# Queries of the linear-attention layers: two row blocks at a time instead of one, in a new order of steps

## The chip, the cores and the metric

The kernel runs on one core of one Trainium2 chip. The metric is the device time of one execution in microseconds (us), as the median of several runs; lower is better. The granted TensorE clock is 1.000 in the profiled execution.

## The reference

Four layers follow one another on one sequence of 2048 rows with 512 columns, in bfloat16: kind A, kind B, kind A, kind B. Each adds its result to its input, and each starts with a layer norm without weights.

```
def _A_ref(x, wqkv, wo):            # first kind: linear attention, 32 heads of 16
    q, k, v = heads(x @ wqkv)
    phi = lambda t: where(t > 0, t + 1, exp(t)) + 1e-6
    pq, pk = phi(q), phi(k)
    kv  = einsum("bhsd,bhse->bhde", pk, v)      # sum over all rows
    z   = einsum("bhsd->bhd", pk)
    num = einsum("bhqd,bhde->bhqe", pq, kv)
    den = einsum("bhqd,bhd->bhq", pq, z) + 1e-6
    return merge(num / den) @ wo

def _B_ref(x, wqkv, wo):            # second kind: causal softmax attention, window of 256 rows
    ...
x = x + _A_ref(_layernorm(x), A_wqkv, A_wo)
x = x + _B_ref(_layernorm(x), B_wqkv, B_wo)
x = x + _A_ref(_layernorm(x), A_wqkv, A_wo)
x = x + _B_ref(_layernorm(x), B_wqkv, B_wo)
```

The sum `kv` runs over all rows, so no output of a layer of the first kind can be formed before all 2048 rows have gone into it. This barrier occurs twice.

## The kernel before

The 2048 rows are cut into 16 row blocks of 128 (`t` = 0 to 15). All activations stay in SBUF: `xres[t]` is the residual stream of block t. The kernel is written as a list of steps (`_Sched.op`), each with an engine, what it reads and writes, and a closure that issues its instructions. `graph` builds the list:

- Part "1.": for each block, `a_kv` does layer norm (`ln`), a transpose of the normed block into `xTa`, the keys `k` with their feature map (`phi`) and the values `v`; `kv_mm` adds the block's product to the sum in PSUM. `sums` (steps `fin0`, `fin1`, L1220) masks the finished sum into `kvz`: the first barrier.
- `segment("2.", ...)`: for each block `a_q` forms the queries of the first layer, `a_out` multiplies them with `kvz` (steps `n0`, `n1`, L942), divides and projects by `Ao` into `xres`; then `b_qkv` and `b_attn` do the second layer on the block. `b_attn` computes scores in units of two pairs of PSUM banks; ScalarE takes the exponential of 1024 columns per pair into `pF` (L1077) or `pH` (L1035); VectorE masks; TensorE multiplies with the values (L1113, L1125).
- Part "2k.": `a_kv` again for the third layer, with the second barrier (`2.fin0`, `2.fin1`) at its end; then `segment("3.", ...)` does the third and fourth layers in the same way.

`a_q` before, for one block: `proj_feat` issues 16 matmuls of 128 columns (steps `q0`, `q1`, L870) into one PSUM bank; `phi` then has four steps on 512 columns: `q.e`, the exponential on ScalarE from PSUM (L879); `q.m`, minimum with 1 and plus 1e-6 on VectorE (L880); `q.r`, the rectifier on ScalarE from PSUM (L882); `q.a`, the sum of both on VectorE (L883). The result lies in one of 18 buffers `pq`.

Work of different blocks and layers is interleaved. What stands in the queue of each engine, and in which order, is fixed by the text `ORDER`: a list of step numbers in the order in which `graph` made them. An apostrophe behind a number takes the second of the engines that the step allows; steps with a choice are the copies out of PSUM (`vc`, `qc`, `kb0`, `kb1`, `zc`), with ScalarE first and VectorE second. Behind a colon stand the buffer slots that the step takes, PSUM banks (0 to 7) among them; a step that takes a buffer waits for all users of the former occupant. Each engine runs its steps strictly in that order and waits by semaphores.

Of the kernel before, what the change touches and what calls it, by code (L numbers as in the profile page):

```python
# [318 lines left out]
def _act_cost(n):  # L319
    return 0.055 + 0.000833 * n  # L320
# [14 lines left out]
230:5.0 194 299 231 184 224:4.0.0 200' 148 207:9 214:7.1 215 300 238:0 271:10 196 195 197 216 208:2.1.3 209 210 180 225 228 284 212 179 278:7.2 279 272:6.2.1  # L335
152 285 286:1 181 301 302:2 314 315 316 169 211 280' 255:11 226 227 229 273 317 213 318:3 256:3.3.2 257 274 239:12 232' 275 25 16 258 259 34 260 23 261 24
262:4.3 263 26 27 246:7.4 240:2.4.0 185 241 247 276 264' 287:13 244 288:5.5.3 201 289 303:14 290 291 310:6.5 311 312' 292 242 248 319:15 294:3.6 277 304:4.7.2
305 308 295 320:5.6.1 306 321 322 324 217 326:2.7 327 243 28 29 17 245 233 249 265 293 307 309 296' 281 297 313 323 328 325 329 330:0 331:1 378:7.4.0 379 380
# [9 lines left out]
658' 671 626 627 672 673 902:6 907:2 684 903 986:0.4.1 987 988 919 449:0 904 955 905:3 881:1 906:3 882:3 883 921:0.6.0 922 923 908 909 685 686:2 687:1 450:5  # L348
884 1407 960:3.0.3 451 961 910:2 911 677:2.1.5 678 912:2 989 962 1408 924 1409 452 474:6.0 475 476 488 477 478:2 479:3 937:3 938 679 933:0.4.1 934 935 674:2.1
675 700 701 1410 932 939 940:1 720 964:0.6.2 702 703 965 966 688:5.0 689 690 691 1411:3 936 942:4 1412:0 941:1 489:0.3 490 943 501 676' 1021:2.6.2 1022 944  # L350
1023 704:0 491 492 493:0 494:1 705:3 967 692:5.2 693 945:2 946 947:0 680 963 721 694' 956:0.2.0 957 958 954 480:4 481 482 644 645 662 1418:7.1 995:0.5.4 996
997 722:1 723:2 1419 1420' 990 913:4 914 915 968:0.2.5 969 970 495:7 496 713:6.2.0 714 715 959 503 497 504:0.0 505 999:4.2.1 1000 1001 972:7 971 977:6 506 973
507 508:3 1056:0.4.0 1057 1058 1024 736 737 974 975:1 738 976:2 978 979 991:0.2.0 992 980:3 981 1421 1422 1423 998 710:7.3 711 712' 993 706:6.1 707 708' 709'
1030:0.4.3 681 716 1031 1032 695:3.1.1 696 994 948:2 1002 1003:0.6.2 697' 1004 949 950 1435 509:3 982:2 510:5 983:4 984 1005 1006 663 1034:0.2.5 1035 985 1036
511 1012:7 512 772 1436 1437 739 1438 740:2 741:4 1060 1007:6 1008 1439:3 1440:2 1424 1449 1450 1091:0.4.1 1092 754 1093 513:3.12.1 514 515 1013 1014 1009
1010:2 1451 517 1011:0 1026:0.4.0 1027 1028 728:2.0 1015:0 1016 1413:3.1.0 1414 1415 729 755 1425:0 1426:1 698 1037 1065:0.6.1 1066 730' 1416 1417 1067
731:5.0.3 732 724:4.2 733 725 1038:0.2.2 1039 1040 1441:7.0.2 1446:6.0 1447 1442 1029 1025 1033 1042:5 1443 1069:0.2.4 1070 1071 726' 1095 1043 727'
1427:4.4.3 1428 1429 699 1452 1448' 1453:1 1041 1047:6 1044 1126:0.2.2 1127 756 1444 1445 1068 746:7.1 747 1017:1 1045:1 1454:5 1046:1 1128 1430 1431 1048
1094 1061:0.4.0 1062 1063 1049 748' 1050:3 1051 757 1052:0 758:2 759:0 1018:3 1019 1100:0.6.3 1101 1102 1020 1465 1466 1467 1460:2.4 773 774 1455:5.3.0 1456
1073:0.3.5 1103 1461 1074 1457 1462 1432:7.3 742:6.3 1433 743 1075 775 1072 1059 1064 1077:2 1078 744 1458 1459 1104:0.4.2 1105 1106 1076 1434' 1079 1082:3  # L360
1083 745' 1080:2 1081:3 516 717 1161:0.6.0 1162 1163 1084 1085:0 764:2.2 765 1086 518 1087:2 766' 1096:0.4.0 1097 1098 1130 749:3.1.2 750 767:2.2.4 776:3 1107
1165 1135:0.6.1 1136 751' 1137 768 769' 1053:5 777:3 1054 1108:0.3.4 1099 1055 1479 760:2.4 761 762' 1468 1109 1110 1111 734 1112:7 1139:0.5.5 1140 1141 1113
1114 763' 1115:1 770 1469:0 1117:4 1118 1116:2 752 1196:0.2.1 519:5.3 1129 520 1197 521 522 1198 523:0 524:3 1119 1120:2 543:7.13.2 544 545 1480 1121 547
# [6 lines left out]
1484:4 1269 1504:4.6 1505 1204 812:0 1240:0.6.3 1241 1242 1158:2 1159 1502 1506' 1503 1510 1160 1523 1192:3 1524 1193:3 1194 1195 1537 807 1213:0.4.4 1214  # L370
813:2 1217:2 1215 1218 1219 1220:1 1221:2 1244:0.6.5 1245 1246 1485:3.7.1 549:4.3 1212 550 551 1538 552 553:3 554:1 1539 1216 1486 1487 1488 1489 818:2.1 819
820 814:1.1 1235 1236:4.6.0 1237 815 816' 1243 1238 821:0.2.0 822 823 1247 1239 1463:5.4 817 1275:2.6.1 1464 1222:0 1223 1224 1276 1277 1248:2.4.2 1249 1525
# [996 lines left out]
```

## Time and profile before

| | |
|---|---|
| median of 3 runs | 421.62 us (420.8 to 422.5) |
| the profiled execution | 422.47 us |
| its span, first to last instruction | 421.1 us |
| outside the span | 1.37 us |
| busy TensorE (PE) | 392.3 us, 93% |
| busy ScalarE (ACT) | 383.6 us, 91% |
| busy VectorE (DVE) | 382.3 us, 91% |
| busy GpSimd (POOL) | 106.0 us, 25% |
| first barrier, last `fin` | 45.0 us |
| second barrier, last `fin` | 252.5 us |

Busy time counts the time in which at least one instruction of the engine is under way. Instructions overlap at their ends: the next one starts before the last one's duration is over, so what an instruction takes of its engine's time is the distance between the starts of back-to-back instructions, and it is shorter than its mean duration.

### The profile page before, as it was taken

The page shows a single profiled execution, that of the slowest core. Times are in us where ns is not written, and L with a number is a line of the kernel's source. Part 1 is how long each engine was busy: PE and PEld are TensorE (multiplying, and loading weights), DVE is VectorE, ACT ScalarE, POOL GpSimd, SP SyncE. Part 2 cuts the span into 40 slices and gives each one's busy share as a digit, 9 for nine tenths or more (in the row PEclk, how much of TensorE's full clock was granted, in tenths as well). Part 3 has the DMA queues.
Part 4 walks back from the last instruction along what each step waited for, and adds up shares of the span by engine and source line. Part 5 has one row for each costly group of instructions (what it writes and reads, how often), then busy time and mean ns, then how long its engine had stood idle before and what let it go on. Part 6 is the DMA issues. An engine that isn't in the chain of part 4 may idle for free.

```text
span 421.1 us, 18887 instructions
## 1 busy us (share of the span) xinstructions
PE 392.3 (93%) x8330; PEld 284.2 (67%) x8404; DVE 382.3 (91%) x1003; ACT 383.6 (91%) x496; POOL 106.0 (25%) x202
## 2 busy tenths in 40 slices
PE   7999989999999899998999999998999899988997
PEld 3655766776766676767586667676767667666675
DVE  7999899999999899998999899999999999978774
ACT  4888679999999999999899767899999999999995
POOL 2230024225232231423131100332322212605200
PEclk9999999999999999999999999999999999999999
DMA  8334426314252130523141201324415422406143
GB/s 265 112 64 138 128 55 126 66 41 99 41 68 43 38 67 16 85 41 59 39 80 22 48 9 39 70 48 68 79 34 80 60 52 33 90 16 117 43 103 92
DMA packets 75720, 29.22 MB, mean 69 GB/s; under 512 B 65264, under 2 KB 73584, under 8 KB 75632
## 3 DMA queue, kind: packets, MB, share of 16 engines
q1 hardware_dynamic: 70336, 22.36, 26.4%
q0 software_dynamic: 4096, 4.46, 5.7%
q8 instruction: 68, 1.11, 1.1%
q10 hardware_dynamic: 1200, 1.11, 0.9%
q14 instruction: 20, 0.16, 0.1%
HBM read 6.29 MB, written 2.10 MB: 20 GB/s over the span
## 4 chain that ended last, share of the span: by engine, by line
PE 42%; ACT 33%; DVE 18%; issue 3%; DMA 3%; POOL 0%; DVEq 0%
ACT pF L1077 23%; PE ps L858 16%; PE ps L870 8%; ACT pH L1035 6%; PE ps L1125 6%; PE ps L1056 5%; PE ps L1113 3%; DVE stats L814 2%; DVE o L954 2%; ACT kbd L971 2%; DMA w_Av<-in_A_wqkv_dram 2%; DVE pF L1095 1%; DVE xres L893 1%; PE ps L916 1%; PE ps L1007 1%
## 5 line engine op out<-in xcount | busy, mean ns | idle before, releaser
L1077 ACT ACTIVATE pF<-ps 128x1024 bf16<-128x1024 f32 x240 | 229.4, 1085 | 4.4 <-PE ps L1056 2.6
L818 POOL TENSOR_TENSOR rstd<-mv,const 128x1 f32<-128x1 f32 x64 | 39.1, 617 | 241.6 <-DVE mv L817 238.6
L981 POOL DMA_DIRECT2D vbd<-vt x128 | 67.1, 532 | 48.2 <-DVE vt L845 30.6
L1035 ACT ACTIVATE pH<-ps 128x1024 bf16<-128x1024 f32 (+1 forms) x64 | 60.3, 1022 | 3.5 <-PE ps L1007 3.2
L1125 PE MATMUL ps<-vbd,pF 128*128 128x34 bf16 x1856 | 60.2, 178 | 2.4 <-issue 2.4
L1125 PEld LDWEIGHTS ps<-vbd,pF 128*128 128x128 bf16 x1856 | 53.3, 96 | 5.5 <-issue 2.7
L1056 PE MATMUL ps<-qT,kbd 32*128 32x128 bf16 x1920 | 48.5, 216 | 5.0 <-ACT pF L1077 2.1
L1095 DVE TENSOR_TENSOR pF<-pF,const 128x512 bf16<-128x512 bf16 (+2 forms) x116 | 46.6, 415 | 3.6 <-ACT pF L1077 3.5
L879 ACT ACTIVATE E<-ps 128x512 bf16<-128x512 f32 x64 | 40.1, 630 | 9.8 <-PE ps L870 6.4
L814 DVE BATCH_NORM_STATS2 stats<-xres 128x6 f32<-128x512 bf16 x64 | 44.0, 689 | 2.0 <-DMA xres<-in_A_x_dram 1.1
L1056 PEld LDWEIGHTS ps<-qT,kbd 32*128 32x128 bf16 x1920 | 28.5, 92 | 22.6 <-ACT pF L1077 9.6
L1043 DVE TENSOR_TENSOR pH<-pH,const 128x1024 bf16<-128x1024 bf16 (+1 forms) x64 | 41.1, 649 | 0.0
L870 PE MATMUL ps<-xT,w_Bq 128*128 128x128 bf16 x512 | 35.5, 219 | 1.0 <-ACT pF L1077 0.7
L870 PE MATMUL ps<-xT,w_Bk 128*128 128x128 bf16 x512 | 35.6, 219 | 0.6 <-ACT pF L1077 0.4
L1113 PEld LDWEIGHTS ps<-vbd,pH 128*128 128x128 bf16 x928 | 29.0, 96 | 8.3 <-issue 2.2
L870 PE MATMUL ps<-xTa,w_Aq 128*128 128x128 bf16 x512 | 34.2, 219 | 0.3 <-DVE pq L883 0.2
L858 PE MATMUL ps<-w_Ak,xTa 128*128 128x512 bf16 (+2 forms) x121 | 32.3, 372 | 1.6 <-issue 0.8
L858 PE MATMUL ps<-w_Av,xTa 128*128 128x512 bf16 (+1 forms) x128 | 32.7, 371 | 1.1 <-issue 0.5
L1113 PE MATMUL ps<-vbd,pH 128*128 128x34 bf16 x928 | 32.7, 178 | 0.9 <-DVE kbd L971 0.3
L858 PE MATMUL ps<-w_Ao,oT 128*128 128x512 bf16 (+2 forms) x119 | 29.4, 354 | 4.2 <-issue 1.6
L870 PEld LDWEIGHTS ps<-xT,w_Bk 128*128 128x128 bf16 x512 | 29.8, 98 | 5.0 <-issue 0.9
L870 PEld LDWEIGHTS ps<-xT,w_Bq 128*128 128x128 bf16 x512 | 29.5, 98 | 5.3 <-issue 2.0
(96 smaller groups left out, 625.6 us busy)
## 6 DMA issues: line engine op xcount, KB each, us to landing
vbd<-vt POOLq DMA_DIRECT2D x128, 34.0 KB, 2.4
xres<-in_A_x_dram SPq DMA_DIRECT2D x16, 128.0 KB, 5.7
out_dram<-xres SPq DMA_DIRECT2D x15, 128.0 KB, 2.3
oT<-o SPq DMA_TRANSPOSE x60, 2.8
w_Ak<-in_A_wqkv_dram ACTq DMA_DIRECT2D x1, 512.0 KB, 5.4
w_Av<-in_A_wqkv_dram ACTq DMA_DIRECT2D x1, 512.0 KB, 6.9
w_Aq<-in_A_wqkv_dram SPq DMA_DIRECT2D x1, 512.0 KB, 7.0
w_Ao<-in_A_wo_dram SPq DMA_DIRECT2D x1, 512.0 KB, 3.9
```

Source lines behind the costliest of these rows:

```text
L814: s.op(n + ".st", {"DVE": 0.595}, lambda e, en: e.bn_stats(a_st, x.h[:]), reads=[x], writes=[st])
L858: i = e.matmul(g.h[:, a:b], xT.h[:, kt, :], w.h[:, kt, a:b], start=(kt == 0), stop=(kt == 3), skip_group_check=True)
L870: i = e.matmul(g.h[:, f * P:(f + 1) * P], w.h[:, kt, f * P:(f + 1) * P], xT.h[:, kt, :], start=(f == 0 and kt == 0), stop=(kt == 3), skip_ ...
L879: s.op(n + ".e", {"ACT": _act_cost(512)}, lambda e, en: e.activation(E.h[:], g.h, ACT.Exp, bias=0.0), reads=[g], writes=[E])
L981: return [e.dma_start(vbd.h[64 * a:64 * a + 64, j, a], vt.h[64 * j:64 * j + 64, a]) for j in range(2)]
L1035: return e.activation(d, c, ACT.Exp, bias=0.0, scale=DH ** -0.5)
L1043: return e.tensor_tensor(v, v, tr, ALU.mult)
L1056: i = e.matmul(ss[r // 2].h[:, r % 2, k * P:k * P + P], kbds[fj[m] // 2].h[32 * r:32 * r + 32, f, fj[m] % 2, :], qT.h[32 * r:32 * r + 32, ...
L1077: s.op("e%d%d" % (u, g), {"ACT": _act_cost(1024)}, lambda e, en, S=ss[g], pb=pb, g=g: e.activation(pb.h[:, 2 * g:2 * g + 2, :], S.h, ACT.E ...
L1095: return e.tensor_tensor(v, v, tr, ALU.mult)
L1113: i = e.matmul(U.h[:, c:c + 34], pH.h[:, 4 * r + f, 64 * a:64 * a + P], vbds[j // 2].h[:, j % 2, :, 4 * f + r, :], start=first[0], stop=Tr ...
L1125: i = e.matmul(U.h[:, c:c + 34], pFs[at[f, m][0]].h[:, r, at[f, m][1] * P:at[f, m][1] * P + P], vbds[fj[m] // 2].h[:, fj[m] % 2, :, 4 * f ...
```

## The change

`a_q` is called for every second block and forms the queries of blocks t and t+1. The weights stay the stationary operand; the moving operand is now 256 columns, 128 from each of the two blocks, so there are 16 matmuls of 256 columns for two blocks in place of 32 of 128. The result takes two adjacent PSUM banks. The four steps of the feature map run on 1024 columns at once, with buffers of their own (`E2`, two of them), and `pq` has 9 buffers of double size. So that one access pattern can reach two blocks, `xTa` is one tile with a fixed place per block instead of a ring of 16 slots. `ORDER` is written anew throughout: 2668 steps in place of 2764 (6 steps of `a_q` fewer for each of 16 pairs of blocks). In it, 62 of the copies out of PSUM (`vc`, `qc`, `kb0`, `kb1`) are on ScalarE in place of 58, the remaining ones on VectorE, and one small copy at the end (`zc0`) moves to ScalarE.

```diff
 ORDER = """
...
-            self.r_xTa = self.ring("xTa", T, [P, 4, P])
+            xTa = self.tiles("xTa", 1, [P, T, 4, P])[0]
+            self.xTa = [_Buf(None, xTa[:, t]) for t in range(T)]
+            self.xTa2 = xTa
...
-            self.r_pq = self.ring("pq", 18, [P, 4, P])
+            self.r_pq = self.ring("pq", 9, [P, 4, 2, P])
+            self.r_E2 = self.ring("E2", 2, [P, 2 * D])
...
-    def a_q(self, xT):
-        pq, E = self.r_pq.buf(), self.r_E.buf()
-        g = self.proj_feat("q", xT, self.w["Aq"], pq, E)
-        self.phi("q", g, E, pq, lambda o: o.h[:].rearrange("p f c -> p (f c)"))
+    def a_q(self, t):
+        pq, E, g, w, xT = self.r_pq.buf(), self.r_E2.buf(), self.pG.buf(2), self.w["Aq"], self.xTa2
+        for part in range(2):
+            def mm(e, en, part=part):
+                for f in (2 * part, 2 * part + 1):
+                    for kt in range(4):
+                        i = e.matmul(g.h[:, part, (f % 2) * 256:(f % 2) * 256 + 256], w.h[:, kt, f * P:(f + 1) * P], xT[:, t:t + 2, kt, :],
+                                     start=(f % 2 == 0 and kt == 0), stop=(kt == 3), skip_group_check=True)
+                return i
+
+            self.s.op("q" + str(part), {"PE": 0.86}, mm, reads=[self.xTa[t], self.xTa[t + 1], w], writes=[g], new=[g, pq, E] if part == 0 else [], tail=0.05)
+        s, gv, out = self.s, lambda: g.h.rearrange("p b c -> p (b c)"), lambda: pq.h[:].rearrange("p f t c -> p (f t c)")
+        s.op("q.e", {"ACT": _act_cost(1024)}, lambda e, en: e.activation(E.h[:], gv(), ACT.Exp, bias=0.0), reads=[g], writes=[E])
+        s.op("q.m", {"DVE": 0.335}, lambda e, en: e.tensor_scalar(E.h[:], E.h[:], 1.0, 1e-6, op0=ALU.min, op1=ALU.add), writes=[E])
+        s.op("q.r", {"ACT": _act_cost(1024)}, lambda e, en: e.activation(out(), gv(), ACT.Relu), reads=[g], writes=[pq])
+        s.op("q.a", {"DVE": 0.6}, lambda e, en: e.tensor_tensor(out(), out(), E.h[:], ALU.add), reads=[E], writes=[pq])
         return pq
...
-                    i = e.matmul(us.h[:, hf, f2 * 136:f2 * 136 + 136], pq.h[:, 2 * hf + f2, :], kvz[hf].h[:, f2, :],
+                    i = e.matmul(us.h[:, hf, f2 * 136:f2 * 136 + 136], pq.h[:, 2 * hf + f2, t % 2, :], kvz[hf].h[:, f2, :],
...
         for t in range(T):
             at(t)
-            pq = self.a_q(xTs[t])
+            if t % 2 == 0:
+                pq = self.a_q(t)
             self.a_out(t, pq, kvz, False, ("o" + n, t) not in BYPE)
...
-            xT, pk, vA = self.a_kv(t, self.r_xTa, ("x1.", t) not in BYPE)
+            xT, pk, vA = self.a_kv(t, self.xTa[t], ("x1.", t) not in BYPE)
```

More of the change, by code (lines that the diff above doesn't have):

```diff
@@ L348 @@
[L348 to L363, printed above, removed]
@@ new lines @@
+591 593:2.2.5 592' 850:4.6.2 851 416:3 560 561 594 852 872 420:0.1 421 422 423 617 618 619 595 424:1 425:1 441:3 442 443 828:5 829 830 823:4 849 824 825 826:0
+831:2 827:0 832 833:0 903:0.6.0 904 906 905 620:2 611:2.0.0 853 612 613' 575:3.1.1 614 842:0.4.3 843 576 577' 844 670 604:7.4 605 606 607 871 841 417:6 615
+418 419 634 635 877:0.2.4 907 878 879 880 453:4.5.0 454 455 457 608:7.0 621:0 845 840 881:0.2.5 882 622:6.5 623 624' 625 636 637 609 883 854:5 855 856 859:4
+860 610' 857:3 938:0.6.1 939 940 578 861 456 458 426:3 862:1 858:3 863 427 638:3 873:0.4.0 874 875 834:2 835 579 864:2 428 652 626:3.1 912:0.6.3 596 913 914
@@ new lines @@
+653 627 639:1 836 1359 654 629:2.0.2 630 655 884 885:0.4.1 886 887 444:6.0 876 445 628' 446 1360 447 448:2 449:3 656:1 657:3 889:3 888 890 459:0.2 460 461 462
+891 631 632 916:4.6.2 917 918 1361 463:1 894:2 895 896 671 942 892:3 897:1 893:0 898 973:0.4.2 974 975 644:7.2 645 1362 646 640:6.0 641 1363:0 908:0.2.0 909
+910 642' 643' 865:5 866 915 450:4 947:0.6.4 948 949 867 1373 451 452 688 689 597 665:5.1.3 666 920:0.2.5 921 667' 922 464:1 465:4 466 1364 1370:7.1 951:0.5.1
+919 1371 899:0 911 924:3 925 467 1374 923 1372' 950 672 673 952 953 929:2 468:0.0 469 470 471 472:3 1008:4.6.0 1009 1010 926 927:2 928:2 1375 930 931 932:3
@@ new lines @@
+933 934:2 706 707 943:0.4.0 944 945 658:3.1 1376 690 659 660' 900:2 982:0.6.3 983 984 661' 708 901 946 902 647:5.2.4 648 955:0.3.2 956 957 941 668 662:2.3 663
+664 649' 650 651 674:2 954 959:7 986:0.5.5 987 960 961 958 964:4 988 473:3 1387 1388 1389 965 962:1 1043:0.2.1 1044 1045 963:1 966 985 967:0 675:2 1377:3 1390
+968 969:1 1391:1 1392 935:7 936 937 978:0.5.0 691 1365:4.0.1 1366 979 980 1378 1011 692:0 1367 683:7.2.1 1401 684 685' 633 686 693:4 676:3.2 1402 1017:0.5.4
+677 1368 1369 977 976 680:7.0 1018 681 682' 1019 1020 474:2 475 1403 1404 678 679 1012 990:0.4.1 1393:6.2.2 1394 1398:7.3 1399 981 994:3 476 991 992 1405:2
@@ new lines @@
+993 1021:0.4.2 989 709 1406 1400' 1379:2.1.0 1380 995 710:1 711:0 999:7 1395 1396 1397 996 997:2 1022 1023 1381 1382 1383 998:0 1078:0.4.2 1079 1080 698:6.1
+699 700' 1000 1013:0.2.0 1014 1015 1024 1001 1002:3 1003 669 1407:6.3.3 1047 1046 1408 1409 1410 1411 724 1052:0.4.3 1053 1016 1412:7.2 1413 1414 694:3.3
+1384:2.0 695 696' 697' 1054 1025:0.6.5 1026 1385 1386' 970:5 971 1027 1028 1056:0.3.1 1004:0 1057 1058 1029:2 1030 1034:7 972 1417 1113:0.5.0 1418 1114 1115
+1031 1082 1032:1 1033:2 1035 1036 1037:0 1048:0.3.0 1038 1049 719:2.0.5 716:5.2 1055 687 720 1087:0.6.4 1059 721' 717 718' 1050 1051 1005:4 722 1006 1007 1431
@@ new lines @@
+1088 1117 1089 1090 725 726 727 1060:0.2.2 1061 712:5.4 713 701:4.1.0 702 1062 714' 1091:0.6.5 1092 1039:2 1093 477:2.6.1 478 479 1064:1 1063 1069:0 728:3
[3 rows of a table added]
+1118:0.4.1 1119 1120 1076 745 1107:2 746:1 1108 737:3.2.2 738 1116 1447 1448 1157:0.6.4 1158 1159 747:3 1077 1428:2.4 492:4.1 493 739' 740 741 1429 1430
+1423:3.4.1 1424 1425 1130:0.6.5 1131 1132 494 495 496:2 497:0 1125 1121 1449:3 1426 752:5.0 753 1427 754' 1129 1152 1133 748:4.0 749 755:3.0.4 756 757' 750
+751 1151 1160 1134:7 1161:0.5.2 1162 1163 1164 1139:4 1140 1135 1218:0.2.0 1219 1220 1136 1137:3 1138:3 498:5 499 500 1141 1142:0 1143 760 761 1153:0.6.3 1222
@@ new lines @@
+1668:5 1669 2138 2141:0.2.5 2142 2143 2093:1 2094:4 1670 2095 2096 1874:7.0 2145:5.0.0 2146 2097:3 2098 2147 2139 2116 1882 1883 1870:4.2 1871 1875 1872' 1873
+1876' 2140 1683:3 2144 1684 1685 1900 2172:5.0.1 2148 2173 2174 1859:7.1.0 1860 1861 2121:4 2122 2123 1701:2.2 1702 1703 1884 1704 2185:0.5.1 2186 2187 2124:0
+1901 1705:2 2125:3 1844 1845 2157:7 1706:0 2158 2159 2160:1 1902 2153:0.2.5 1885 2161:0 1886:2 1887:1 2154 2155 1862 1863 2175 2126:4 2127 2152 2128 2129:3
+2130 2131:1 2177:6.0.0 2178 2179 1692:5 1693 1877:4.2.1 2181:2.6.2 2176 2182 2183 1694 1878 2156 2162:5 2163 1879' 2208:0.2.2 2209 2210 1918 2180 2164 2165:2
@@ new lines @@
+1919 2166 1903 1904:1 2184 1707:4 1710:6.0 1708 1709 1711 1892:5.1 2221:0.2.3 2222 1712 2223 1713 1714:2 1893 1894' 2132:4 2133 2134 1936 2189:0.6.4 2190
+2193:5 2194 2195 2191 2099:2 2224 2188 1937 2213:0.2.5 2214 2196:1 2215 1748 2192 2197:3 1895:4.0.3 1715:3 1896 1897' 1898 1920 1921 1888:7.3 1889 2217:0.5.0
+2212 1725:2.3 1726 1890 1891 1727 1728 1729:1 2100:4 2101 2102 1716:7 1922:3 2216 2218 1717 1718 2219 2220 2244:0.2.0 2245 2246 2198:4 2199 2200 2201:2 2202
+1880 2257:0.6.2 2258 2259 1954 1905:3 1913:5.1.5 1955 1938 1734:2.0 2167:0 1735 1736 1737 1738:2 1910:4.2 1911 1730:1 1912 2247 1914 2225:0.6.1 2226 2227
@@ new lines @@
+1915' 1906:3.4 2211 1731:2 1732 1733 2249:0.4.4 2250 2251 1907 1908' 1909' 1923:2 1749:6.1 1750 1751 2203:2 1881 2229:2 2230 2231 2232:3 2253:0.4.5 2254 2255
+1752 2233:0 2204:3 2205 1753:1 2103 2228 2206 1739:3 1931:2.2.2 2280:0.6.1 2281 2282 1772 2256 1932 1933' 1924:5.5 1925 1926' 1927' 2248 1972 1939 1973
+2293:0.3.0 2294 2295 2234:2 2235 2236 2237:2 2238 1940:0 2285:0.6.3 2286 2287 1916 2252 2260 1928:5.3 1740:4 1741 1742 2261:0.2.1 1929 1930' 1899 2265:7 2266
[5 rows of a table added]
+1993 1994:3 1995:3 1964:2.1 2361:0.4.1 2362 2363 1965 2008 1966' 2239:2 2360 2356 2339 2340:2 2341:1 2388:0.6.1 2389 2390 2342:2 2343 2344 2401:0.4.3 2402
@@ L431 @@
+2536 2545:0.2.1 2546 2547 2486:7 2053' 2487 2488 2489:0 2513:0.4.2 2490 2514 2515 2025 2517:6 2518 2519 2537:0.2.4 2538 2539 2348:7 64 2349 2350 2541:4.0.0
[7 rows of a table added]
 """
@@ L535, in general @@
         self.xres = [_Buf(None, v.h) for v in self.xres]
+        self.xTa = [_Buf(None, v.h) for v in self.xTa]
         xv = self.x[0].rearrange("(t p) d -> t p d", p=P)
@@ L563, in general @@
             for t in range(self.T):
-                self.a_out(t, self.a_q(self.ln("ln", t, self.r_xT, False)), kvz, False, False)
+                self.ln("ln", t, self.xTa[t], False)
+                if t % 2:
+                    pq = self.a_q(t - 1)
+                    self.a_out(t - 1, pq, kvz, False, False)
+                    self.a_out(t, pq, kvz, False, False)
             s.at = ("gb", 0)
@@ L825, in transp @@
         s = self.s
-        o = ring.buf()
+        o = ring if isinstance(ring, _Buf) else ring.buf()
+        held = [o] if o.pool else []
         if dma:
-            s.op(n, {"SP": 1.25}, lambda e, en: e.dma_start_transpose(o.h[:], src.h[:]), reads=[src], writes=[o], new=[o], dma=True)
+            s.op(n, {"SP": 1.25}, lambda e, en: e.dma_start_transpose(o.h[:], src.h[:]), reads=[src], writes=[o], new=held, dma=True)
             return o
@@ L836, in tr @@
             return i
-        s.op(n, {"PE": 0.38}, tr, reads=[src, self.ident], writes=[g], new=[g, o])
+        s.op(n, {"PE": 0.38}, tr, reads=[src, self.ident], writes=[g], new=[g] + held)
         self.copy(n + "c", o, g, lambda: (o.h[:], g.h.bitcast(BF)[:, 0:D].rearrange("p (f c) -> p f c", f=4)))
@@ L1304, in graph @@
             s.at = ("2k.", b1 + t)
-            xT, pk, vA = self.a_kv(t, self.r_xTa, ("k2.", t) not in BYPE)
+            xT, pk, vA = self.a_kv(t, self.xTa[t], ("k2.", t) not in BYPE)
             xTs2.append(xT)
```

65 lines of the change are left out of this document (15 added, 50 removed), and 85 rows, old and new, of the table ORDER.

## The prediction

> **What bounds the kernel now.** I read the page first, for the busy shares and the chain of waits. In the fence, the first line gives busy time per engine and the second the engines along the chain that ended last.
>
> ```profile
> PE 392.3 (93%) x8330; PEld 284.2 (67%) x8404; DVE 382.3 (91%) x1003; ACT 383.6 (91%) x496; POOL 106.0 (25%) x202
> ...
> PE 42%; ACT 33%; DVE 18%; issue 3%; DMA 3%; POOL 0%; DVEq 0%
> ```
>
> Three engines are almost equally full and the chain changes between them, so an average does not say which one ends last. I therefore took busy time by stretches: of 30 us, and of 4 us around the second barrier (252.5 us). The columns are stretch, length, then busy PE, weight loads, DVE, ACT, POOL with counts.
>
> ```profile
> 36.00:40.00 4.00, 4.00 (x26) 2.11 (x25) 3.96 (x15) 3.58 (x8) 0.00 (x0) 1.00 0.34 89
> ...
> 120.00:150.00 30.00, 28.24 (x654) 20.43 (x657) 27.74 (x67) 29.20 (x35) 7.96 (x16) 1.00 0.30 51
> 150.00:180.00 30.00, 28.26 (x651) 20.79 (x655) 28.61 (x74) 28.79 (x37) 7.77 (x15) 1.00 0.35 53
> ...
> 248.00:252.00 4.00, 4.00 (x57) 3.27 (x56) 3.93 (x11) 2.06 (x4) 0.00 (x0) 1.00 0.02 4
> 264.00:268.00 4.00, 3.82 (x70) 3.15 (x67) 3.90 (x11) 3.14 (x6) 1.24 (x3) 1.00 0.46 85
> ...
> 300.00:330.00 30.00, 28.44 (x672) 20.03 (x676) 28.84 (x71) 29.90 (x36) 5.70 (x11) 1.00 0.42 59
> 330.00:360.00 30.00, 28.05 (x771) 21.80 (x778) 28.26 (x72) 29.80 (x34) 9.23 (x18) 1.00 0.26 48
> ```
>
> PE is full ahead of both barriers. From 60 to 236 us all three stand at 94 to 97%, ACT a little ahead. DVE is full in the 20 us behind the second barrier (3.90 of 4). From about 276 to 405 us ACT alone ends last (29.8 to 29.9 of 30).
>
> **Durations.** By form, the rows that the change touches or that are nearest (mean ns last before the bar):
>
> ```profile
> L870 PE MATMUL ps<-xTa,w_Aq 128*128 128x128 bf16 x512 | 34.2, 219 | 0.3 <-DVE pq L883 0.2
> L882 ACT ACTIVATE pq<-ps 128x512 bf16<-128x512 f32 x32 | 19.7, 623 | 1.9 <-PE ps L870 1.9
> L883 DVE TENSOR_TENSOR pq<-pq,E 128x512 bf16<-128x512 bf16 x32 | 13.2, 414 | 0.4
> L1043 DVE TENSOR_TENSOR pH<-pH,const 128x1024 bf16<-128x1024 bf16 x56 | 37.9, 682 | 0.0
> L1187 PE MATMUL ps<-w_Bo,oT 128*128 128x256 bf16 x8 | 1.5, 276 | 0.0
> ```
>
> Means contain the overlap with the next instruction, so I cost by the distance between starts. The timeline of ACT shows it for 512 columns (first column the start), the chain for longer runs:
>
> ```profile
> 253.08 0.62 ACT L879 ACTIVATE E<-ps 128x512 bf16<-128x512 f32 x1
> 253.56 0.63 ACT L882 ACTIVATE pq<-ps 128x512 bf16<-128x512 f32 x1
> 254.03 0.64 ACT L879 ACTIVATE E<-ps 128x512 bf16<-128x512 f32 x1
> ```
> ```profile
> 17.16 0.89 PE ps L870 x16
> ...
> 349.80 9.17 ACT pF L1077 x10
> ```
>
> **The merge itself.**
> - ACT: 512 columns take 0.477 us start to start, 1024 take 0.904 (the commonest distance in L1077). A pair of blocks has two merged steps, each saving 2 x 0.477 - 0.904 = 0.050. 16 pairs x 2 x 0.050 = 1.6 us.
> - DVE, `q.a`: 0.335 for 512; for 1024 the row L1043 gives 0.601, so 0.069 is saved. `q.m`: 0.201 for 512; no row has it at 1024. It costs between 0.20 (no growth) and 0.40 (twice); I take 0.333, that is the 0.069 fixed part of L883's kind plus twice the rest, since both run on bfloat16 from SBUF. 16 x (0.069 + 0.069) = 2.2 us, ends 1.1 and 4.3.
> - PE: 16 products of 128 columns take 0.89, so a pair takes 1.79. For 256 columns the starts in L1187 lie 0.109 apart, so 16 take 1.74: 0.05 saved per pair, 0.8 us in all. Ends: nothing, or 1.1 if 256 cost half of the 0.215 of 512 columns.
>
> [...] The rows here show 50 ns (0.477 and 0.904 us start to start). [...]
>
> **Edits at nothing.** The fixed `xTa` tiles add no wait: a block's tile is rewritten for the third layer only after that block has passed the second layer, long after its query product; without that cover it would cost one transpose landing. 9 double `pq` hold as much as 18 single ones. Block t's query now also waits for block t+1's transpose; only the first pairs, ahead of 45 us, are near it, where PE has key and value products to run.
>
> **The order.** Counting the step numbers of both orders, up to the first `n0` behind the second barrier five more copies go to ACT (15 to 17 `kb`, 5 to 7 `qc`, 6 to 3 `vc` of the second layer, 16 to 20 `vc` of the A layers), each about 0.48 to 0.57 on ACT against 0.60 to 0.66 on DVE. Behind it one goes back (and `zc0` to ACT). Whole sums: ACT -1.6 + 1.9 + 0.2 = +0.5 us; DVE -2.2 - 2.5 = -4.7; PE -0.8. By stage, with every queued step at its start-to-start time:
> - Up to the last `kv` of the first layer PE is full, with four blocks of queries ahead of it either way: no change.
> - Up to the second barrier's first `n0`: PE -0.7, ACT -0.5, DVE -5.7. The least is -0.5, the most -5.7. All three are at 94 to 97% there, and each waits for the others, so I take the mean, -2.3.
> - From there to the first score step of the fourth layer: DVE is full and carries between -0.2 and +0.5 (two query steps fall behind the barrier): +0.3.
> - The ACT-full rest: one `kb` pair of copies fewer, one `qc` more, `zc0` more, less overlap of queries with it: -0.8.
>
> Sum: -2.3 + 0.3 - 0.8 = -2.8 us. Against the profiled execution: span 421.1 - 2.8 = 418.3, plus 1.37 around it, 419.7. That execution (422.47) lies 0.85 above the median of 421.62, so the time to expect is 421.62 - 2.8 = **418.8 us**. What the new neighbours in the queues do to idle time shows in no row. In equal 30 us stretches of the second layer ACT's busy time varies by about 0.2 to 0.4 us around its mean; over some 10 such stretches an estimate of 2 to 3 us either way, which goes into the range.
>
> **Rivals.**
> 1. *Nothing measurable.* Where ACT ends last, only ACT's sum counts, and it rises by 0.5; where PE does, 0.8 goes. Then 420.8 to 422.1, middle **421.3**. For it: ACT's 29.8 of 30 in a third of the span. Against: its idle before 276 us, some of which waits for DVE's copies.
> 2. *Slower: the pair of banks.* A single query block held one of 8 banks; a pair now takes two adjacent ones from the first product to the end of `q.r`: 1.74 + 2 x 0.904 + two hand-overs of about 0.2, nearly 4 us. A score unit takes two pairs, so of four pairs three remain, and copies and sums need the last: the next unit can't be filled while ACT empties this one. Price: a unit refilled only after release costs ACT about 0.65 (its 0.40 row of 16 matmuls and hand-over), two units per hold, 1.3 us. Six pairs stand among the score units of the second layer (10, 12, 14 and, of the third layer, 2, 8, 0), so at most 7.8 us. It decides above 2.8 / 6 = 0.47 us per pair. At two thirds of the price, 421.6 - 2.8 + 5.2 = **424.0**. For it: score waits on a bank that ACT frees are the largest PE waits now,
>
> ```profile
> PEld ps L1056 <- ACT pF L1077: 9.6, 34, 0.6
> ...
> ACT pF L1077 <- PE ps L1056: 2.6, 8, 0.5
> ```
>
> Against it: ACT itself waited only 2.6 us for scores (second line).
> 3. *The merge does not pay:* 256 columns in two runs of 128 cost twice 128. That takes 0.8 us from PE's sum alone: 419.6, within the forecast's spread.
>
> **How the numbers follow.** About 0.5%, 2.1 us, is what a measurement of this kernel can tell from no change. The forecast with gains over 2.1 us has 0.44 (414 to 419.5). Case 1 has 0.33, the smaller gains of the forecast included (419.5 to 423.7). Case 2 has 0.23. The range runs from 414.0 (DVE's sum decides up to the barrier, -5.7 - 0.5, and 1.4 of the order) to 424.8 (rival 2 at its two thirds and a little above).
>
> **What would show it.** Right: DVE's busy time down by about 4 to 5 us, ACT's level, the second barrier's `fin` near 250 us, L882 at 16 instructions of about 1.07 us, the query products at 16 per 1.74 us. Wrong: waits of ACT L1077 for L1056 well above 2.6 us, or of weight loads L1056 for ACT above 9.6, in the stretches with a query pair (rival 2); the `fin` still at 252 us with DVE emptier (rival 1).

## The result and the profile after

| | before | after |
|---|---|---|
| median | 421.33 us (5 runs, 420.8 to 422.5) | 425.43 us (5 runs, 424.79 to 426.92) |
| ratio, 95% interval | | 1.0086 [1.0066, 1.0105] |
| the profiled execution | 422.47 us | 424.79 us |
| its span | 421.1 us | 423.5 us |

The changed kernel is slower by 4.1 us. That is outside the range of the prediction (414.0 to 424.8) and on the other side of its forecast. The two profiled executions differ by 2.3 us only: that of before is the highest of its five runs, that of after the lowest.

The page of the kernel after, busy time per engine and engines along the chain:

```profile
PE 392.4 (93%) x8079; PEld 279.8 (66%) x8154; DVE 377.9 (89%) x966; ACT 383.6 (91%) x469; POOL 107.2 (25%) x202
...
ACT 41%; PE 33%; DVE 20%; issue 3%; DMA 2%; SPq 1%; POOL 0%; DVEq 0%; POOLq 0%
```

DVE is 4.4 us emptier (382.3 to 377.9) and ACT is level, as forecast, in a span that is 2.4 us longer. The chain lies more on ACT (41%, 33% before) and less on PE (33%, 42%), without being shorter. PE's busy time cannot be compared here: these two traces lack 75 and 74 matmul records (8079 of 8154 after, 8330 of 8404 before), and the complete traces further below show 401 us. What the groups by form say of the merge itself:

```profile
L935 PE MATMUL ps<-xTa,w_Aq 128*128 128x256 bf16 x256 | 31.3, 273 | 0.9 <-DMA w_Aq<-in_A_wqkv_dram 0.5 <-DVE pq L944 0.2
L943 ACT ACTIVATE pq<-ps 128x1024 bf16<-128x1024 f32 x16 | 16.7, 1047 | 0.3 <-PE ps L935 0.3
L941 ACT ACTIVATE E<-ps 128x1024 bf16<-128x1024 f32 x16 | 16.7, 1043 | 7.0 <-PE ps L935 7.0
L944 DVE TENSOR_TENSOR pq<-pq,E 128x1024 bf16<-128x1024 bf16 x16 | 10.8, 675 | 0.3
L942 DVE TENSOR_SCALAR E<-E 128x1024 bf16<-128x1024 bf16 x16 | 6.6, 413 | 0.0
```

32 instructions have become 16 in each group. By the distance between starts the products take 0.109 us, `q.e` and `q.r` 0.903 and 0.904, `q.a` 0.60 and `q.m` 0.333: each as the prediction priced it, the one unknown (`q.m`) included.

The same stretches as before (last three numbers: granted clock, DMA share, GB/s). The second barrier is later now, so its stretch is 250 to 254:

```profile
36.00:40.00 4.00, 3.95 (x20) 1.78 (x19) 2.69 (x10) 3.17 (x7) 0.00 (x0) 1.00 0.77 219
120.00:150.00 30.00, 27.88 (x590) 19.77 (x596) 27.57 (x62) 28.84 (x35) 6.12 (x11) 1.00 0.24 48
150.00:180.00 30.00, 27.92 (x676) 20.83 (x681) 26.16 (x67) 29.21 (x34) 8.64 (x15) 1.00 0.33 58
250.00:254.00 4.00, 4.00 (x38) 3.05 (x36) 3.93 (x12) 2.37 (x5) 0.00 (x0) 1.00 0.00 0
264.00:268.00 4.00, 3.48 (x45) 2.77 (x45) 3.80 (x12) 2.78 (x5) 0.67 (x2) 1.00 0.05 10
300.00:330.00 30.00, 28.50 (x668) 20.69 (x674) 29.10 (x71) 28.79 (x34) 7.34 (x14) 1.00 0.43 65
330.00:360.00 30.00, 27.04 (x729) 20.34 (x732) 28.49 (x73) 29.98 (x35) 6.76 (x13) 1.00 0.33 57
```

DVE's relief is there (26.16 of 30 from 150 to 180 us, 28.61 before), but ACT is not fuller for it: 28.84 and 29.21 against 29.20 and 28.79. Between 300 and 330 us ACT, which was full with 29.90, has 28.79.

The view of the tile `kvz` gives the second barrier (the two numbers behind the durations are the starts of the first and the last instruction). Its last `fin` (L1236) started at 252.5 us before and should have been near 250:

```profile
L958 PE MATMUL ps<-kvz,pq x128: 219/223/233, 46.4 to 343.8; 128*128 128x136 bf16 x128
...
L1236 DVE TENSOR_TENSOR kvz<-kvacc,const x2: 433/437/441, 254.3 to 255.0; 128x272 bf16<-128x272 f32 x2
```

It starts at 255.0. The first products with `kvz` start at 46.4 us, 45.3 before. Starts of landmarks in both traces (the differences are taken before rounding):

| | before | after | later by |
|---|---|---|---|
| first `n0`, first barrier | 45.3 | 46.4 | 1.1 |
| first score product of layer 2 | 60.1 | 60.7 | 0.5 |
| first score product of its last block | 224.9 | 225.9 | 1.0 |
| first `n0` behind the second barrier | 252.8 | 254.9 | 2.1 |
| first score product of layer 4 | 266.9 | 269.7 | 2.8 |
| first score product of its last block | 403.4 | 406.0 | 2.6 |
| end of the span | 421.1 | 423.5 | 2.4 |

The time is lost ahead of the first barrier, ahead of the second and behind it. In the long middle, from 60 to 225 us, VectorE has 4.0 us less to do (155.0 before, 151.0 after), nearly all that was taken off it, and the middle is no shorter for it (164.8 us before, 165.2 after). At the first barrier the timeline of PE (start, duration) showed one block of query products in front of the first `n0` before,

```profile
44.40 1.06 PE L870 MATMUL ps<-xTa,w_Aq 128*128 128x128 bf16 x16
45.29 0.87 PE L942 MATMUL ps<-kvz,pq 128*128 128x136 bf16 x12
```

and shows a whole pair after:

```profile
44.68 1.91 PE L935 MATMUL ps<-xTa,w_Aq 128*128 128x256 bf16 x16
46.43 0.64 PE L958 MATMUL ps<-kvz,pq 128*128 128x136 bf16 x8
```

And the waits (total us, times, longest) that the prediction named as signs of rival 2, the pair of banks:

```profile
PEld ps L1072 <- ACT pF L1093: 10.4, 38, 0.6
...
ACT pF L1093 <- PE ps L1072: 3.3, 7, 0.9
```

Both signs have risen by under a microsecond (9.6 to 10.4, 2.6 to 3.3). Neither accounts for 4 us.

### The profile page after: what moved, and what is told of

Read it like the earlier page. It is cut to its first block, busy times and chain, and to the rows that moved or that the text cites. A ratio compares the mean times of both kernels' runs of the same rounds, so it can differ in the third digit from the quotient of the medians.

```text
span 423.5 us, 18313 instructions
## 1 busy us (share of the span) xinstructions
PE 392.4 (93%) x8079; PEld 279.8 (66%) x8154; DVE 377.9 (89%) x966; ACT 383.6 (91%) x469; POOL 107.2 (25%) x202
## 4 chain that ended last, share of the span: by engine, by line
ACT 41%; PE 33%; DVE 20%; issue 3%; DMA 2%; SPq 1%; POOL 0%; DVEq 0%; POOLq 0%
ACT pF L1093 28%; PE ps L862 11%; ACT pH L1051 8%; PE ps L1141 5%; PE ps L1072 4%; PE ps L874 4%; DVE stats L817 3%; PE ps L1129 3%; ACT kbd L987 3%; PE ps L935 2%; DVE o L970 2%; DMA w_Aq<-in_A_wqkv_dram 2%; DVE pk L889 1%; PE ps L1023 1%; DVE xres L897 1%
## 5 line engine op out<-in xcount | busy, mean ns | idle before, releaser
L821 POOL TENSOR_TENSOR rstd<-mv,const 128x1 f32<-128x1 f32 x64 | 40.5, 647 | 198.6 <-DVE mv L820 196.9
L1072 PEld LDWEIGHTS ps<-qT,kbd 32*128 32x128 bf16 x1920 | 28.6, 92 | 23.9 <-ACT pF L1093 10.4
L862 PE MATMUL ps<-w_Av,xTa 128*128 128x512 bf16 (+2 forms) x126 | 33.0, 369 | 1.0 <-issue 0.5
L862 PE MATMUL ps<-w_Bv,xT 128*128 128x512 bf16 (+2 forms) x129 | 30.5, 345 | 2.6 <-issue 1.5
L862 PE MATMUL ps<-w_Ak,xTa 128*128 128x512 bf16 (+2 forms) x123 | 31.2, 370 | 1.4 <-issue 0.3
L935 PE MATMUL ps<-xTa,w_Aq 128*128 128x256 bf16 x256 | 31.3, 273 | 0.9 <-DMA w_Aq<-in_A_wqkv_dram 0.5
```

What stands on the lines that cost most here:

```text
L821: s.op(n + ".rs", {"POOL": 0.53}, lambda e, en: e.tensor_tensor(a_rs, v, self.half.h[:], ALU.pow), reads=[mv, self.half], writes=[rs])
L862: i = e.matmul(g.h[:, a:b], xT.h[:, kt, :], w.h[:, kt, a:b], start=(kt == 0), stop=(kt == 3), skip_group_check=True)
L1072: i = e.matmul(ss[r // 2].h[:, r % 2, k * P:k * P + P], kbds[fj[m] // 2].h[32 * r:32 * r + 32, f, fj[m] % 2, :], qT.h[32 * r:32 * r + 32, ...
```

## The experiments

The expectations number their theories. In words: the new order loses time and the merge gains a little (theory 1); the larger pieces cost the time (theory 2); the pair of query products ahead of the first `n0` costs it (theory 3); pairs leave any order less room (theory 4), because one block is taken away from where it fitted (4a) or because of the two adjacent banks and the larger pieces (4b, rival 2 among them); any new order loses against that of before (theory 5). Beside them it was under trial whether relief of one engine returns less than the mean of three engines, with which the prediction summed. Every ratio is against the kernel before, on the same chip.

**The merge undone in place.** The order, the buffers and the two banks of the kernel after stay (inside a `pq` buffer the two blocks now lie one behind the other); every step of a pair issues two blocks one after the other, with the instructions of before.

```diff
-  s.op("q.e", ..., lambda e, en: e.activation(E.h[:], gv(), ACT.Exp, bias=0.0), ...)
+  s.op("q.e", ..., two(lambda e, b: e.activation(Eh(b), gv(b), ACT.Exp, bias=0.0)), ...)
...  # q.m, q.r, q.a alike; the products with 128 columns per block
```

> The changed kernel with its order and buffers, but every step of a pair issues the two blocks one after the other: 32 products of 128 columns, two 512-column instructions each for q.e, q.m, q.r and q.a. Theory 1 (the merge pays its sum, the new order lost more): undoing the merge in this order costs about the third part of 0.8 + 1.6 + 2.2 us that is felt where three engines are equally full, 1.5 us: 427 us, 1.3% above the kernel before, DVE busy time up by 2 us. Theory 2 (the larger pieces are what costs): the smaller pieces take the 4 us back, at least 2 of them: 421 to 423 us.

426.34 us, 1.0113 [1.0088, 1.0138]. Its page:

```profile
PE 401.5 (94%) x8410; PEld 283.7 (67%) x8410; DVE 380.0 (89%) x998; ACT 385.9 (91%) x501; POOL 106.8 (25%) x202
```

Against the kernel after DVE has 2.1 us more and ACT 2.3: about the sums of the merge (2.2 and 1.6). The time differs by 0.9 us (426.34 - 425.43), and the intervals of the two ratios overlap. So the merge does not cost the 4 us: undoing it gave none of them back, where the theory of the larger pieces expected at least 2. It probably gains a little where it stands. The new order with its pairs of banks, but without the merge, costs 5.0 us (426.34 - 421.34).

**The first barrier.** In the order of after, the second half of the query products of the pair ahead of the first `n0`, and the exponential behind them, move behind the first four `n` steps.

```diff
 ORDER:  ... steps q1 and q.e of blocks 2 and 3
-  ahead of the first n0
+  behind the n0 and n1 of blocks 0 and 1
```

> The changed kernel with one move: at the first barrier the second half of a query pair (q1 of blocks 2 and 3, 0.87 us of TensorE) goes behind the first four n products instead of ahead of them. Theory 3 (a query pair of 1.74 us stands in front of the first product behind the barrier, where a single block of 0.89 us stood): the first n product starts near 45.8 us instead of 46.4, and what of that 0.6 us reaches the end shows how much of a late barrier the rest takes up: 424.8 to 425.4 us. Theory 2 says the same of this run; theory 1 says no change at the end, 425.4 us.

425.74 us, 1.0101 [1.0075, 1.0126], no gain over after. In its profile the first `n0` starts at 45.6 us, 0.9 earlier than in after, but the first score product at 62.3, 1.6 later. From 52 to 55.5 us that execution has half the granted clock. Four more of its six runs have the same mean clock, 0.996; the one run at full clock took 424.57. What this is comes below. With one such run, the 1.1 us at the first barrier are neither shown nor excluded as a part of the loss.

**What relief of one engine returns.** Three kernels in the order of before, each with less work on one engine. `s_dve` runs `q.m` on one column; `s_act` runs `q.r` on 256 of 512 columns; `s_pe` leaves out one of four parts of the query products.

```diff
-  e.tensor_scalar(E.h[:], E.h[:], 1.0, 1e-6, ...)                  # q.m
+  e.tensor_scalar(E.h[:, 0:1], E.h[:, 0:1], 1.0, 1e-6, ...)        # s_dve
-  e.activation(view(o), g.h, ACT.Relu)                             # q.r
+  e.activation(view(o)[:, 0:256], g.h[:, 0:256], ACT.Relu)         # s_act (q.a adds E to E)
-  for kt in range(4):                                              # q0, q1
+  for kt in range(3 if w is self.w["Aq"] else 4):                  # s_pe
```

> The kernel before, in its own order, with the queries' q.m on one column instead of 512 (the minimum and the 1e-6 are left out of the other 511): 32 instructions of 0.20 us shrink to about 0.06, so VectorE carries 4.4 us less, about what the change takes off it. The forecast's step (a third of VectorE's saving reaches the end) gives -1.5 us: 419.8. The rival (VectorE's sum decides nothing, its order and the waits do) gives at most -0.4: 421 us.

> The kernel before, in its own order, with q.r on 256 of 512 columns and q.a adding the exponential to itself (the rectified part is left out): ScalarE carries 32 x 0.213 = 6.8 us less, the other engines the same. By the forecast's mean of three engines -2.3 us: 419 us. If ScalarE is the bound wherever queries run in the second layer, about -4: 417. If it decides nothing there, 421 us.

> The kernel before, in its own order, with the queries' products over 3 of 4 parts of the columns (a quarter of the sum is left out): TensorE carries 128 x 0.056 = 7.2 us less. By the mean of three engines -2.4 us: 418.9. If TensorE is the bound around both barriers, where 20 of 32 query blocks run, about -4.5: 417. If it decides nothing, 421 us.

| | work taken away | time | ratio | returned per us, 95% |
|---|---|---|---|---|
| s_dve | 4.4 us of DVE | 421.09 (before 422.19) | 0.9973 [0.9959, 0.9987] | 0.26 [0.12, 0.39] |
| s_act | 6.8 us of ACT | 421.70 | 0.9984 [0.9972, 0.9996] | 0.10 [0.02, 0.17] |
| s_pe | 7.2 us of PE | 420.70 | 0.9955 [0.9939, 0.9971] | 0.26 [0.17, 0.36] |

The work taken away is the number of instructions times the difference of the distances between starts; the last column is the ratio's share of 422.19 us over it. All three returned less than the third that the mean of three engines gives, but only ACT's interval excludes a third. For ACT, the fullest engine by the stretches (29.90 and 29.80 of 30 us between 300 and 360 us), the line of `s_act`'s page shows how the relief is lost:

```profile
PE 400.7 (95%) x8404; PEld 284.2 (68%) x8404; DVE 381.6 (91%) x1003; ACT 377.5 (90%) x496; POOL 106.0 (25%) x202
```

Against the page of before ACT's busy time falls by 6 us, and the median time by 0.5: in this order ACT waits where it worked. If the three add, which was not measured, the merge (PE 0.8, ACT 1.6, DVE 2.2) brings 0.2 + 0.16 + 0.57 = 0.9 us by these rates. That is the difference which undoing it in place measured, though both are uncertain by about half of it.

**Other orders.** To see whether the loss belongs to pairs or to any new order, orders were made by many small moves of single steps, kept where a sum over the steps' costs and waits did not end later. The costs and waits in that sum are figures of the kernel's text, not of the chip. `drift1` and `drift2` make 600 such moves at random from the order of before; `single_x1` and `single_x2` rework the whole order with single query blocks; `pair_x1` and `pair_x2` do so with pairs, from the order of after and from that of before. `slots` keeps the order of before and only lets the buffer slots be assigned anew: 117 of 845 steps get another slot.

```diff
 ORDER = """
-37 4 0 3 6 7 1 8 9 2 68 61:7 69 70 5 67 71 72:0 73:6.0 62 38 66 85 86 87 10 39 40 88 41   # before
+37 4 0 3 6 7 1 8 9 2 68 61 69 70 5 67 71 72 73 62 38 66 85 86 87 10 39 40 88 41           # slots
+4 0 6 37 7 1 8 9 68 2 61 69 70 5 3 71 72 67 73 62 38 66 85 86 10 87 39 40 41 42           # drift1
+37 3 6 2 67 0 7 1 8 5 4 39 9 38 68 69 70 66 71 61 72 41 40 85 86 73 34 87 88 33           # single_x1
...
```

> The kernel before with its order of steps as it is; only the buffer slots that stand behind colons are dropped, so that each step takes the free slot that comes free first (117 of 845 steps get another slot, PSUM banks among them). It is the base line for the two runs beside it. Theory 1 (an order is tuned to the chip step by step, and any other one costs): 421 to 422.5 us, since the order is kept. If slots alone cost as much as the change (425 us), it is not the order of steps but the choice of banks.

> The kernel before with 600 random single moves in its order, none of which lets the order's own due times end later: 69 of 977 TensorE steps, 41 of 500 ScalarE steps and 253 of 998 VectorE steps get a new neighbour ahead of them. Theory 5 (the order of before fits the chip beyond what step costs say, so that any new order loses): 1 to 3 us above the run with dropped slots. Otherwise: within 0.7 us of it, and then what is lost in the changed kernel belongs to its own placing of query pairs.

> As the run with 600 random moves, from another random start: 79 of 977 TensorE, 42 of 500 ScalarE and 275 of 998 VectorE steps get a new neighbour. If the loss of 2.5 us there is what any new order pays (theory 5), 423 to 425 us again; if it was one unlucky move, 421.5 to 422.5 us.

> The kernel before (single blocks) with its order changed by the same kind and number of small trials. It bounds what an order alone can do here. Theory 1: about 1 us above the pairs made the same way, 419 to 421 us. Theory 4: 2 us or more below them, 417 to 419 us. If this is 421 us too, such trials move nothing on the chip and neither theory is touched by these runs.

> As the last, a second order of single blocks from an independent run of trials. Its distance from the first says how far two such orders lie apart on the chip; theories 1 and 4 expect the same of it as of the first.

> The changed kernel (queries in pairs) with another order: the changed kernel's order, with single steps and short runs of steps moved and engine choices of copies flipped over many thousand small trials, each kept where the kernel's own step costs and due times said that it ends no later. Theory 1 (the merge gains about 1 us, the order of the changed kernel alone lost 5): a better order takes the pairs to 420 us or below, and below single blocks with an order made in the same way. Theory 4 (pairs leave any order less room: two adjacent banks, pieces of 0.9 to 1.8 us): the pairs stay at 421.5 to 424, 2 us or more above single blocks.

> The changed kernel (queries in pairs) with an order made the same way from the other end: the order of the kernel before, the two blocks' steps replaced by one pair at the place of one of them, then the same small trials. Theory 1: near 420 us. Theory 4: 422 to 425 us. If it lands more than 2 us from the first such order, orders alone scatter by that much.

| | time | before | ratio |
|---|---|---|---|
| slots | 421.66 | 421.77 | 0.9995 [0.9984, 1.0006] |
| drift1 | 423.59 | 421.77 | 1.0054 [1.0034, 1.0073] |
| drift2 | 423.57 | 422.60 | 1.0026 [1.0011, 1.0041] |
| single_x1 | 424.32 | 423.15 | 1.0041 [1.0020, 1.0061] |
| single_x2 | 424.86 | 423.15 | 1.0072 [1.0043, 1.0101] |
| pair_x1 | 426.02 | 423.15 | 1.0067 [1.0048, 1.0085] |
| pair_x2 | 430.20 | 423.15 | 1.0165 [1.0144, 1.0186] |

Slots cost nothing. Each of the six other orders is slower than that of before, with pairs or without, though on paper none ended later than the order it started from. The gains that the reworked orders were expected to bring did not come, so the expectations of both sides failed in their times. In `drift1` 69 of 977 TensorE steps and 253 of 998 VectorE steps have a new predecessor, and it already loses 0.5%. Of the orders reworked in the same way, those with pairs took 1.2 to 5.9 us more than those with single blocks. That is the sign that theory 4 (pairs leave an order less room) expected and theory 1 did not. But the two orders with pairs lie 4.2 us apart, so two of each kind are few.

**Pairs against displacement.** `mix5` is the order of before with 5 of the 16 pairs merged (blocks 0 and 14 of the first layer's queries, 0, 2 and 10 of the third's, each with its successor); all other steps keep their order. In `moved5` the queries of the same blocks stand at the same places, but each block alone, with its own bank and its own single instructions. `mix5_un` is `mix5` with its steps issued block by block, and `pair_x1_un` is `pair_x1` so.

```diff
 # mix5
-  pq = self.a_q(xTs[t])
+  if (n[0], t - t % 2) not in PAIRS:
+      pq = self.a_q1(t)          # one block, as before
+  elif t % 2 == 0:
+      pq = self.a_q(t)           # two blocks
 # moved5: a_q as before, ORDER alone moves; E of the moved blocks from a ring of its own
+  self.r_Eq = self.ring("Eq", 4, [P, D])
```

> The kernel before, order kept, but for 5 of 16 pairs of query blocks (blocks 0 and 14 of the first segment, 0, 2 and 10 of the second, each with its successor) the two blocks are merged into one pair at the place of one of them, as the change does; the other 22 blocks stay single. Theory 1 (the merge itself gains): 5 x 0.06 = 0.3 us less than the run with dropped slots. Theory 4 (a pair has to pull one block's steps 30 to 460 places away from where they fit, and takes two adjacent banks at once): 1 us or more per pair above it, 425 us or more.

> The kernel before with the same five pairs of blocks as in the run with five pairs merged, moved to the same places in the order, but every block keeps its own 128-column products, its own 512-column steps and a single PSUM bank; the other blocks' order is kept. If the price of five pairs comes from pulling one block's steps away from where they fitted (theory 4a), this is as slow as that run: 429 to 431 us, plus 0.3 for the steps that are not merged. If it comes from the two adjacent banks and the large pieces (theory 4b), 422 to 424 us.

> The run with five pairs merged, with its order, its pairs of banks and buffers, but the two blocks issued one after the other within each step. Against that run it shows the merge by itself: by the sums and by what each engine's relief brought in the kernel before, 5 x 0.06 = 0.3 us slower, 430.8 us; against the run with moved single blocks it shows the pair of banks by itself.

> The first of the two other orders for pairs, with the two blocks issued one after the other within each step. A second measure of the merge by itself in a fixed order: theory 1 says 0.9 us slower than with merged steps (426.0), so 426.9 us; if merging costs because of its larger pieces, it is faster.

| | time | before | ratio |
|---|---|---|---|
| mix5 | 430.52 | 421.77 | 1.0208 [1.0180, 1.0235] |
| moved5 | 431.45 | 422.60 | 1.0250 [1.0203, 1.0298] |
| mix5_un | 431.04 | 422.60 | 1.0202 [1.0173, 1.0231] |
| pair_x1_un | 428.88 | 422.60 | 1.0166 [1.0137, 1.0195] |

Five pairs cost 8.8 us, and the same five displaced without any merge and without a pair of banks cost as much (`moved5`, 8.9 us), as theory 4a expected. By the runs at full clock alone the costs are 7.8 us for `mix5`, 8.5 for `moved5` and 8.4 for `mix5_un`. So for these five pairs neither the two banks nor the longer instructions are the price; the displacement is. The pages of `slots` (the order of before) and then of `moved5` show the same work, each within 1 us:

```profile
PE 401.5 (95%) x8404; PEld 284.4 (68%) x8404; DVE 381.8 (91%) x1003; ACT 383.3 (91%) x496; POOL 106.4 (25%) x202
```
```profile
PE 401.5 (93%) x8403; PEld 284.8 (66%) x8403; DVE 382.7 (89%) x1003; ACT 384.2 (89%) x496; POOL 106.5 (25%) x202
```

and the spans are 420.6 and 429.8 us. Two waits carry part of the 9.2 us, in `slots`:

```profile
DVE dn L1126 <- PE ps L1116: 5.4, 9, 1.1
ACT pF L1068 <- PE ps L1047: 2.1, 6, 0.6
```

and in `moved5`, whose lines are two higher:

```profile
ACT pF L1070 <- PE ps L1049: 7.5, 15, 1.0
DVE dn L1128 <- PE ps L1118: 7.0, 10, 1.6
```

ACT waits for scores 7.5 us instead of 2.1; DVE waits 7.0 us instead of 5.4 for the products with the values. In `mix5` the wait of ACT is 4.5 us, in the kernel after 3.3: it is one place of the loss, not all of it.

Of the displaced steps some stand later than before, others earlier. By the starts of `q.e`, the farthest move takes block 3 of the third layer from 177 to 257 us, to just ahead of the second barrier; block 15 of the first layer goes from 167 to 154 us. `moved5` is 0.7 us behind `slots` at the first score product of layer 2, 1.2 at that of block 10 (149 us), 5.9 at that of block 15 (223 us), 7.0 at the first `n0` behind the second barrier and 9.2 at the end. Which of the five pairs costs how much was not tried singly.

Between `pair_x1` and `pair_x1_un` the ratios differ by 1.0% (1.0067 and 1.0166), some 4 us. But all six runs of `pair_x1` had the full clock and four of the five of `pair_x1_un` had not, so this is not the merge alone; the one at full clock (428.51) is 0.7% above `pair_x1` by the ratios. Between `mix5` and `mix5_un` nothing can be told (1.0208 and 1.0202). Whether the merge returns more in one order than in another is not shown.

**Half clock.** Not all runs of these kernels had a mean granted clock of 1.0. `pair_x2` shows what happens, in stretches of 1 us (PE's busy time is the third number, the granted clock the third from the end):

```profile
66.00:67.00 1.00, 1.00 (x32) 0.84 (x30) 1.00 (x4) 1.00 (x3) 0.68 (x2) 1.00 1.91 111
67.00:68.00 1.00, 0.27 (x4) 0.08 (x2) 0.97 (x4) 1.00 (x3) 0.35 (x1) 1.00 0.30 81
68.00:69.00 1.00, 0.00 (x0) 0.00 (x0) 0.80 (x2) 0.16 (x1) 0.00 (x0) 1.00 1.02 175
69.00:70.00 1.00, 0.45 (x2) 0.30 (x4) 0.00 (x0) 0.00 (x0) 0.00 (x0) 0.54 0.54 77
70.00:71.00 1.00, 1.00 (x8) 0.31 (x10) 0.00 (x0) 0.00 (x0) 0.00 (x0) 0.50 0.81 228
71.00:72.00 1.00, 1.00 (x38) 0.91 (x38) 0.89 (x2) 0.36 (x1) 0.00 (x0) 0.50 1.24 333
72.00:73.00 1.00, 1.00 (x18) 0.90 (x19) 0.50 (x1) 1.00 (x2) 0.00 (x0) 0.76 1.37 153
```

PE pauses for 2.3 us (67.3 to 69.6), and from 69.1 to 72.5 us, for 3.4 us, its granted clock is half. All 89 runs of the kernel before that stand beside these experiments, and all 42 of `slots` and the three `s_` kernels, had a mean clock of 0.999 or more. Of the 88 runs with a new order, the kernel after among them, 28 had 0.991 to 0.996; one such fall, half of 3.4 us in some 425, lowers the mean of a run by 0.004, and the profiled execution of `pair_x2` has 0.996. In `drift1` the seven runs without it have a median of 423.33 us, the four with it 425.25: 1.9 us. It is a price that a new order can bring, but not the main one: four of the five runs of after had the full clock, at a median of 425.42, and `drift1` without it is still 1.6 us above the kernel before.

## Why the prediction was wrong

- **The terms of the merge: right.** 0.050 us per merged ACT step, 0.069 each for `q.m` and `q.a` and 0.05 per pair on PE stood in the trace as priced, DVE's busy time fell by 4.4 us against a forecast of 4.7, ACT stayed level. The 0.050 is twice the 0.477 us between starts for 512 columns less the 0.904 for 1024.
- **The order at "2 to 3 us either way": the step that failed.** What the new neighbours in the queues do was put at nothing in the sum, and into the range as a spread to both sides. That spread was worked out from how ACT's busy time scatters between stretches of one order, which says nothing of another order. The runs showed a cost in its place: 5.0 us for the new order with the merge undone. The six other new orders, with pairs or with single blocks, all lost too: two random drifts 1.0 and 1.8 us by the medians. Five pairs of blocks, displaced, lost 8.8. No new order that was tried gained.
- **The kernel's own sum over the new order is not in the prediction.** `_Sched.schedule` adds the kernel's own step costs along `ORDER`, with waits and buffers. Its `span` is 413.9 us for the order of before and 416.1 for that of after, with the merged costs: 2.2 us later, the right sign and half of the size. For `slots`, `mix5` and `moved5` it is 415.1, 422.2 and 423.2. It is a warning and no forecast: for the four reworked orders it gives 409.9 to 414.3, and all of them were slower on the chip.
- **The stages.** At the nearest landmarks of the two profiled executions, which lie 2.3 us apart:

| | forecast | measured |
|---|---|---|
| up to the first `n0` | 0 | +1.1 |
| to the first `n0` behind the second barrier | -2.3 | +1.0 |
| to the first score product of layer 4 | +0.3 | +0.7 |
| the rest | -0.8 | -0.4 |
| sum | -2.8 | +2.4 |

- The first row was put at "no change" because PE is full and four blocks of queries stand ahead of the last `kv` either way. That count is right, but behind the last `kv` two blocks now stand in front of the first `n0`, where one stood. Whether this 1.1 us reaches the end stays open. The largest miss is the second row, 3.3 us.
- **The mean of three engines: too large.** "All three are at 94 to 97% there, and each waits for the others, so I take the mean" prices every relief at a third. The runs with one engine relieved returned 0.26 (DVE), 0.10 (ACT) and 0.26 us (PE) per us. By these rates the whole change, DVE -4.7, ACT +0.5, PE -0.8, is worth -1.2 + 0.05 - 0.2 = -1.4 us, half of the -2.8. This is the smaller part of the miss: 1.4 of the 6.9 us between -2.8 and +4.1.
- **The second barrier near 250 us: wrong sign.** It started at 255.0 with DVE emptier. The prediction had listed 252 with DVE emptier as the sign of rival 1, but not that PE, which is full ahead of the barrier in both kernels (4.00 of 4), would reach it later.
- **Rival 2, slower by the pair of banks: wrong mechanism.** Its 424.0 us lies near the result, but its signs moved by 0.8 and 0.7 us, and for five pairs displacement without a second bank cost the same as with it. That 424.0 lies near 425.4 is luck: the sign of the result was in the prediction, its cause was not.
- **Rival 3, 256 columns in two runs of 128 cost twice 128: wrong.** Starts lie 0.109 us apart, as with one run of 256.

**Open.** How the 5 us of the new order divide among the first barrier, the stretch ahead of the second and the displaced query blocks is not settled: moving half of the pair off the first barrier met the half clock. That banks cost nothing was shown with five pairs in the order of before, not in the order of after. Nor was it found what makes the order of before better than other orders of the same work; no version here beats the kernel before.

## What to carry to other kernels

Where several engines stand at over 90% in a fixed order, price saved work by what its relief returns, measured by leaving some of it out, and not by the sum or the mean of the busy times: here 0.1 to 0.26 us per us. A rewritten order is a term of its own. The ones that were reworked or drifted here all lost, 0.3 to 1.7% for the same or less work, so do not put it at zero in the sum. Run the kernel's own sum of step costs on it first, and measure it alone, with the saved work undone in place. Merging two blocks takes one of them away from the place that it fitted: compare with the same displacement without the merge before blaming the merged instruction.

## What the runs showed of the hardware

TensorE's granted clock fell to half (0.50) for 3.4 us after a stretch in which it was not idle throughout. In the four profiles with such a fall (those in the last microsecond of a span left aside) PE had been busy 38% (`mix5_un`), 47% (`pair_x2`), 47% (`e_n0first`) and 53% (`pair_x1_un`) of the 3.4 us ahead of it. The emptiest such stretch in the kernel before, behind its start-up, is 69%. Low shares do not always bring it: the profiled executions of `single_x1` and `drift2` have stretches of 41% and 51% without such a fall behind them. The longest pauses of PE ahead of the four falls were 1.0 to 2.3 us. The same kernel shows the lower mean clock in some runs only: in `drift1` 4 of 11, in `e_n0first` 5 of 6. What brings the fall is not shown.
